# k of a pair in one load, first masks from ScalarE's queue, fewer zero products, counts behind a burst, an own h bank for the last block's odd chunks

## The chip, the cores and the metric

One core of a Trainium2 chip runs the kernel alone. Its engines are TensorE (PE: matmul, with the weight load shown as PEld), VectorE (DVE), ScalarE (ACT), GpSimd (POOL) and SyncE (SP), which here only issues DMAs. The metric is the device time of one execution in microseconds (us).

## The reference

Three stages follow each other; what is computed is this, with B, H, S, D = 4, 8, 576, 64 and 2304 tokens of 512 numbers.

```python
scores = np.matmul(q, k.transpose(0, 1, 3, 2)) / np.sqrt(D)
mask = (rel >= 0) & (rel < 128)                  # rel = query position - key position
scores = np.where(mask, scores - slope[h] * abs(rel), -1e9)
attn = softmax(scores)                           # exp of score - max, over its sum + 1e-9
x = (attn @ v), heads side by side               # [2304, 512]

h = x @ w_in                                     # [2304, 2048], w_in and w_out in double precision
g = s * np.maximum(h, 0) ** 2 + b
x = (g @ w_out).astype(np.float32)               # [2304, 512]

do = x @ w_skip > 0                              # 1360 of the 2304 rows with these inputs
e = argmax(x @ w_gate), gate = softmax(x @ w_gate)[e]      # 8 experts
out = x;  out[do] += gate * (np.maximum(x[do] @ w1[e], 0) @ w2[e])
```

With these inputs the experts 0 to 7 get 639, 194, 63, 83, 51, 20, 167 and 143 rows, which is 5, 2, 1, 1, 1, 1, 2 and 2 tiles of 128 rows.

## The kernel before, in words

**Attention** works on units: one batch, one pair of heads, and one of two halves of the queries. A unit has two or three groups (128 queries of the pair, against up to 256 keys). For a group, `qk` makes the scores of both heads (TensorE, `s_ps`), `low` adds the mask and finds the row's limit (VectorE, L179), `soft` takes exp (ScalarE, L187), sums, inverts (L189, L190) and multiplies (L196 on VectorE, L194 on ScalarE), `tr` transposes the result (TensorE, `t_ps`), `tr_ev` copies it out (ScalarE), and `pv` multiplies by v (`o_ps`). The product of `low` and `soft` is the tile `tp`, of which there are two buffers: `low` of group i+2 waits until `tr` has read group i.

The first 12 groups (phase 0) run as steps, `attn_step`, before any block of the next stage. `load_unit` issues a unit's q, k, v from SyncE's queue, the masks among the first three units, in the order of the code: for unit 0 in two pieces. k lies in memory once for each half of the partitions, so that the array holds each head's k twice in a row (`_arrays`). Ahead of the first group stand five products of zeros (`idle`), and five more follow `attn_step(2)`, each after the last score product by an issue-after mark (L703).

**The dense stage** has 6 blocks of 384 tokens, and each block 16 chunks m of 128 hidden units. `g1` makes the hidden chunk (12 products into the bank `h`, `h_ps`), ScalarE takes relu (L485), VectorE the square times s (L486), and `g1_split` splits it in a high and a low part (L495 on ScalarE, L496 on VectorE). `g2` adds the previous chunk's 9 products to the accumulators `acc0` to `acc2`. Weights come as 64-bit words and are split by `w_split` on VectorE (L412, L414, L416, L77) and ScalarE (L419): seven pieces during the attention steps 6 to 12, the rest within block 0. Attention of the later phases is woven into the blocks 0 to 4 by `events`: a `burst` (scores of two groups, `pv2` of the two before) and then a `turn` for each group (transpose and copy), at places that are fractions of the block's chunks.

**Routing** of block j-1 (`logits`, `route`) runs in block j. `route` stops half way at a `yield`: the counting products (`p_ps`, two small matmuls in the bank `at`, the same bank as `t_ps`) come later, in block j+1 behind `g1` of chunk 1. VectorE reads `p_ps` at L619 and L621.

**The experts** follow in `moe2`: expert weights stream through buffers (`ring`, `more`), are split by ScalarE (L681) and VectorE (L77), and each expert runs either `single` (one tile) or `pair` (two tiles), chosen by a branch on its count. `x_t` transposes gathered rows into the bank `p_x` (L835). `FURTHER` says how many copies of the two-more-tiles body stand in the code behind a branch that is taken only when an expert has more tiles than its first pair.

The order on an engine is set by a list scheduler, in part from its own time estimates; a chain of issue-after marks (`mm`, `order`) fixes most of TensorE's order from block 0 on, and `moe2` is scheduled by hand from `wide(0)` on. Of the change, these lines of before are touched:

```python
for c0, c1 in ((0, 128), (128, 384)) if u == 0 else ((0, 384),):   # unit 0 in two pieces
...
for _ in range(5):                                                  # zero products behind step 2
...
ts = [at + n_seg / n * f for f in ((0.55, 1) if j else (0.65, 0.85))]
...
i = g1_part(m, (3,) if j == 0 and m < 2 else range(4))              # bank "h" always
...
if counting and m == 1:
    next(counting, None)
...
x_t(rows1[0], 1)                                                    # into p_x
```

Of the kernel before, what the change touches and what calls it, by code (L numbers as in the profile page):

```python
# [17 lines left out]
B, H, S, D = 4, 8, 576, 64  # L18
# [4 lines left out]
NB = NT // TB  # L23
# [6 lines left out]
UB = 3  # L30
CONV = (6, 7, 8, 9, 10, 11, 12)
LAST = NE - 1
FURTHER = (2, 0, 0, 1, 0, 0, 0, 0)

# [6 lines left out]
def body(tc, q_in, k_in, vl, wm, we, wg, wgt, s_in, b_in, mask_in, cst_in, rout_in, ids_in, out):  # L43
    nc = tc.nc
# [11 lines left out]
    cst = main.tile([128, 4, 128], F32, name="cst")  # L56
# [27 lines left out]
    NQ, K0, NK = (384, 192), (0, 256), (384, 320)  # L84
    units, groups, ends = [], [], []
# [17 lines left out]
    def load_unit(u):  # L103
        if u >= len(units):
            return
        b, pair, half = units[u]
        q = A.tile([128, NQ[half]], F32, name="q", tag="q", bufs=UB)
        k = A.tile([128, NK[half]], F32, name="k", tag="k", bufs=UB)
        vt = A.tile([128, 2, 3, D], F32, name="vt", tag="vt", bufs=UB)

        for c0, c1 in ((0, 128), (128, 384)) if u == 0 else ((0, 384),):
            cq, ck = slice(c0, min(c1, NQ[half])), slice(c0, min(c1, NK[half]))
            nc.sync.dma_start(out=q[:, cq], in_=q_in[b, pair, :, half * 384 + cq.start:half * 384 + cq.stop])
            for i in range(2):
                rows = slice(64 * i, 64 * i + 64)
                uload[u] = nc.sync.dma_start(
                    out=k[rows, ck], in_=k_in[b, 2 * pair + i, rows, half * 384 + ck.start:half * 384 + ck.stop])
            if u < 3 and c0 == 0:
                hs = slice(2 * u, 2 * u + 2 if u < 2 else H)
                nc.sync.dma_start(out=masks[:, hs], in_=mask_in[hs].rearrange("h p n -> p h n"))  # L120
        us[u] = q, k, vt
        if u == 0:
            nc.sync.dma_start(out=cst[:, 0], in_=cst_in[:, 0])

        late.append(lambda: nc.sync.dma_start(
            out=vt, in_=vl[b, 2 * pair:2 * pair + 2, :, half * 3:half * 3 + 3].rearrange("h p t d -> p h t d")))
        while late and u:
            late.pop(0)()
# [216 lines left out]
    def events(j, n_seg):  # L345

        first, last = (ends[j] // 2, ends[UNTIL[j]] // 2)
        n, ev, wait = last - first, [], 0
        if j == 0:
            wait = 2  # L350
            n_seg -= wait
            ev.append((wait, turn, groups[2 * first - 1]))
        for i in range(n):
            d, at = first + i, 1 + wait + i * n_seg / n
            ev.append((at, burst, d))
            gs = groups[2 * d:2 * d + 2]
            ts = [at + n_seg / n * f for f in ((0.55, 1) if j else (0.65, 0.85))]
            if ceil(ts[0]) == ceil(ts[1]):
                ev.append((ts[1], turn2, gs))
            else:  # L360
                ev += [(t, turn, g) for t, g in zip(ts, gs)]
        return sorted(ev, key=lambda e: e[0])
# [116 lines left out]
        return i  # L479

    def g1(j, m):
        i = g1_part(m, (3,) if j == 0 and m < 2 else range(4))
        hp = hs[m]
        r = M.tile([128, TB], F32, name="r", tag="r", bufs=1)
        nc.scalar.activation(out=r, in_=hp, func=ACTF.Relu)  # L485
        nc.vector.scalar_tensor_tensor(out=r, in0=r, scalar=sb[:, 0:1], in1=r, op0=ALU.mult, op1=ALU.mult)  # L486
        gt[j, m] = r
        return i
# [209 lines left out]
    for i in range(ends[0]):  # L698
        attn_step(i)
        if i == 2:  # L700
            for _ in range(5):
                with tc.issue_after(pe['q'].ins):
                    pe['q'] = nc.tensor.matmul(idle[:, 0:128], lhsT=zero, rhs=zero, start=True, stop=True)  # L703
        if i == 8:
            nc.sync.dma_start(out=cst[:, 1:], in_=cst_in[:, 1:])
            nc.sync.dma_start(out=sb[:, 0:1], in_=s_in.unsqueeze(0).to_broadcast([128, 1]))
            nc.sync.dma_start(out=sb[:, 1:2], in_=b_in.unsqueeze(0).to_broadcast([128, 1]))
            nc.sync.dma_start(out=rc, in_=rout_in)
            nc.sync.dma_start(out=ids, in_=ids_in)
            nc.sync.dma_start(out=wg_sb, in_=wg)  # L710
        w_fetch()
        while w_at[1] < len(CONV) and CONV[w_at[1]] <= i:
            w_step()
# [6 lines left out]
    nc.gpsimd.memset(fill[:, 1::2], 0)  # L720
    nc.sync.dma_start(out=lst.rearrange("(p n) c -> p (n c)", p=128), in_=fill)

    counting = None
    for j in range(NB):
        if j:
            split_x(j)
        if j == NB - 1:
            ast.close()
            R = mk("moe2", ast, side="right", reuse_waits="tile")
            ws.free.extend(R.tile([128, 1024], F32, name=f"ring{i}") for i in range(RING))  # L730
            pump()
            later = moe2(tc, locals_ns(locals())).send
        todo = events(j, 2 * NM - 2) if j < UNTIL[j] else []

        def attn_until(k):
            while todo and todo[0][0] <= k:
                _, f, what = todo.pop(0)
                f(what)

        for m in range(NM):  # L740
            if j == 0:
                w_need(m)
                if m == 0:

                    g1_part(0, range(3))
                    with tc.issue_after(pe['o'].ins):
                        i = g1_part(1, range(3), "acc0")
                    order[0] = i.ins
            i = g1(j, m)
            if counting and m == 1:  # L750
                next(counting, None)
                counting = None
            attn_until(2 * m + 1)
            done = g1_split(j, m)
            if j == 0:
                w_step()
            if m:

                if j == NB - 1 and m == NM - 1:
                    g2(j, m - 2, (1, 2))  # L760
                g2(j, m - 1, (0,) if j == NB - 1 and m == NM - 2 else (0, 1, 2))
            elif j:
                g2(j - 1, NM - 1)
                evac(j - 1)
            attn_until(2 * m + 2)
            if j == 0:
                w_step()
            if j and m >= 1:
                n = 2 if j < NB - 1 else 3

                with tc.issue_after(done.ins):
                    for i in range(min(9 * TPB, n * m - n), min(9 * TPB, n * m)):
                        logits(j - 1, i)
                if m == (NM - 1 if j < NB - 1 else 10):
                    counting = route(j - 1)
                    next(counting, None)
            if j == NB - 1 and m in (10, 15):
                later(None)
            if j == NB - 1:
                split()  # L780
# [28 lines left out]
def moe2(tc, L):  # L809
# [147 lines left out]
    def pair(e, rows0, rows1, k):  # L957

        left = rest(e if e == 0 else e - 1)
        own = [p for p in NEED[e] if p[0] == e] if e else []  # L960
        x_t(rows1[0], 1)
        conv(own, 2)
        second(e - (e > 0))
        fin(1, *left)
# [188 lines left out]
```

## Time and profile before

| | |
|---|---|
| median of 3 runs | 742.35 us (739.86 to 742.79) |
| profiled execution | 742.56 us; its span 740.8 us, so 1.76 us lie around the span |
| TensorE busy | 718.6 us, 97% of the span |
| VectorE busy | 522.1 us, 70% |
| ScalarE busy | 373.9 us, 50% |
| GpSimd busy | 62.7 us, 8% |
| DMA | 96.42 MB, mean 130 GB/s |

The stages in time: attention steps from 0 to about 44 us, block 0 to about 135 us, blocks 1 to 5 to about 544 us, experts to about 730 us, and then the end of the program. An engine's busy time is the time covered by its instructions; matmul ends are modelled, so what tells most of TensorE are the gaps between its instructions, and by how much a product starts later than the one before it lets it.

### The profile page before, as it was taken

How to read it: one execution, taken by the hardware profiler on the slowest of the kernel's cores; microseconds unless marked ns; L12 is line 12 of the kernel's file. 1: busy time of each engine (PE TensorE's matmuls, PEld its weight loads, DVE VectorE, ACT ScalarE, POOL GpSimd, SP SyncE). 2: the span in 40 equal slices, each digit the busy share in tenths (PEclk: the TensorE clock that was granted, in tenths of full speed). 3: DMA queues.
4: the chain of work that ended last, by engine and by line, in shares of the span. 5: the costliest groups of instructions: out<-in, count | busy, mean ns of one | idle time of the engine just before them, and what ended most of it. 6: DMA issues, size and time to landing. Idle time of an engine off the chain costs nothing. (4 is left out here: it accounts for less than half of the span.)

```text
span 740.8 us, 13066 instructions
## 1 busy us (share of the span) xinstructions
PE 718.6 (97%) x4552; PEld 616.5 (83%) x4552; DVE 522.1 (70%) x1544; ACT 373.9 (50%) x889; POOL 62.7 (8%) x67
## 2 busy tenths in 40 slices
PE   8789999999999999999999999999999999999995
PEld 6468888888888888788888888898888889887994
DVE  4999999667777676777777665699744253999341
ACT  5776777544554444555555332454442133888230
POOL 0000000000001000000000100010105301322011
PEclk9789999999999999999999999999999999999998
DMA  7897342522314121432223111456463532999000
GB/s 194 263 345 228 128 119 54 155 65 84 94 56 131 54 68 54 132 93 70 70 80 111 30 43 31 158 170 170 127 201 81 214 114 70 344 367 386 13 22 17
DMA packets 51360, 96.42 MB, mean 130 GB/s; under 512 B 8938, under 2 KB 26858, under 8 KB 51264
## 3 DMA queue, kind: packets, MB, share of 16 engines
q1 hardware_dynamic: 46192, 86.35, 36.8%
q0 software_dynamic: 3296, 5.60, 2.4%
q10 hardware_dynamic: 1776, 3.28, 1.2%
q8 instruction: 50, 0.82, 0.5%
q14 instruction: 46, 0.38, 0.2%
HBM read 84.89 MB, written 13.65 MB: 133 GB/s over the span
## 5 line engine op out<-in xcount | busy, mean ns | idle before, releaser
L145 PE MATMUL h_ps<-xh,wh 128*128 128x384 f32 x378 | 130.9, 346 | 0.7 <-ACT r L485 0.7
L145 PE MATMUL h_ps<-xl,wh 128*128 128x384 f32 x378 | 127.5, 337 | 0.1
L145 PE MATMUL h_ps<-xh,wl 128*128 128x384 f32 x378 | 127.3, 337 | 0.0
L485 ACT ACTIVATE r<-h_ps 128x384 f32<-128x384 f32 x96 | 47.0, 490 | 134.6 <-PE h_ps L145 113.1
L486 DVE SCALAR_TENSOR_TENSOR r<-r,sb 128x384 f32<-128x384 f32 x96 | 59.1, 616 | 59.1 <-ACT r L485 58.6
L547 DVE CUSTOM_DVE_ANT_0 junk<-x,hp 128x512 bf16<-128x512 f32 x135 | 92.8, 687 | 1.6
L145 PE MATMUL acc<-wh,gh 128*128 128x512 f32 x288 | 87.0, 410 | 0.0
L187 ACT ACTIVATE tp<-tp,stat 128x256 f32<-128x256 f32 (+2 forms) x160 | 74.7, 469 | 19.8 <-DVE stat L179 19.7
L145 PE MATMUL acc<-wh,gl 128*128 128x512 f32 x288 | 83.0, 396 | 0.0
L145 PE MATMUL acc<-wl,gh 128*128 128x512 f32 x288 | 82.5, 394 | 0.0
L495 ACT ACTIVATE gh<-r,sb 128x384 fp32r<-128x384 f32 x96 | 59.2, 616 | 41.5 <-DVE r L486 40.9
L496 DVE SCALAR_TENSOR_TENSOR gl<-r,sb,gh 128x384 fp32r<-128x384 f32 x96 | 59.0, 615 | 28.2 <-ACT gh L495 28.0
L145 PEld LDWEIGHTS h_ps<-xh,wh 128*128 128x128 f32 x378 | 71.0, 188 | 6.8 <-issue 2.7
L145 PEld LDWEIGHTS h_ps<-xl,wh 128*128 128x128 f32 x378 | 71.1, 188 | 3.1 <-DVE xl L77 0.4
L145 PEld LDWEIGHTS h_ps<-xh,wl 128*128 128x128 f32 x378 | 70.9, 188 | 0.0
L145 PEld LDWEIGHTS acc<-wh,gl 128*128 128x128 f32 x288 | 54.0, 189 | 13.6 <-DVE gl L496 0.9
L145 PEld LDWEIGHTS acc<-wl,gh 128*128 128x128 f32 x288 | 54.1, 188 | 12.6
L655 POOL DMA_INDIRECT lst<-pay,di x18 | 18.5, 1028 | 489.9 <-DVE di L652 486.0
L179 DVE CUSTOM_DVE_ANT_0 tp<-s_ps,masks 128x256 f32<-128x256 f32 (+2 forms) x160 | 52.6, 377 | 9.6 <-PE s_ps L143 4.1
L145 PEld LDWEIGHTS acc<-wh,gh 128*128 128x128 f32 x288 | 50.3, 190 | 7.8 <-issue 2.9
L870 PE MATMUL p_o<-wh,hth 128*128 128x512 f32 x120 | 48.6, 405 | 0.3 <-ACT hth L886 0.2
L870 PE MATMUL p_o<-wl,hth 128*128 128x512 f32 x120 | 47.4, 395 | 0.0
(170 smaller groups left out, 1256.0 us busy)
## 6 DMA issues: line engine op xcount, KB each, us to landing
w_words<-wm SPq DMA_DIRECT2D x30, 512.0 KB, 6.3
more<-we SPq DMA_DIRECT2D x30, 512.0 KB, 6.6
ring<-we SPq DMA_DIRECT2D x28, 512.0 KB, 4.5
hp<-wgt SPq DMA_DIRECT2D x45, 256.0 KB, 3.3
vt<-vl SPq DMA_DIRECT2D x32, 192.0 KB, 3.0
x2d<-x SPq DMA_DIRECT2D x17, 256.0 KB, 2.9
out<-x SPq DMA_DIRECT2D x17, 256.0 KB, 2.8
more<-we ACTq DMA_DIRECT2D x6, 512.0 KB, 6.1
```

What stands on the lines that cost most here:

```text
L145: i = f(*args, **kw)
L179: anchor['v'] = nc.vector.tensor_tensor_reduce(out=t[0:nr, i, c0:c0 + n], in0=ps[i][0:nr, c0:c0 + n], in1=masks[0:nr, 2 * units[u][1] + i, ...
L187: anchor['s'] = nc.scalar.activation(out=t[0:nr, i, c0:c0 + n], in_=t[0:nr, i, c0:c0 + n], func=ACTF.Exp, scale=-1.0, bias=st[0:nr, 0, i:i ...
L485: nc.scalar.activation(out=r, in_=hp, func=ACTF.Relu)
L486: nc.vector.scalar_tensor_tensor(out=r, in0=r, scalar=sb[:, 0:1], in1=r, op0=ALU.mult, op1=ALU.mult)
L495: nc.scalar.activation(out=gh, in_=r, func=ACTF.Identity, bias=sb[:, 1:2])
L496: i = nc.vector.scalar_tensor_tensor(out=gl, in0=r, scalar=sb[:, 1:2], in1=gh.bitcast(F32), op0=ALU.add, op1=ALU.subtract)
L547: nc.vector.tensor_tensor_reduce(out=junk, in0=x2t[j, t], in1=w, scale=1.0, scalar=0.0, op0=ALU.mult, op1=ALU.add, accum_out=lgs[j][:, t, ...
L655: i = nc.gpsimd.indirect_dma_start(out=lst, out_offset=bass.IndirectOffsetOnAxis(ap=di[:, t:t + 1], axis=0), in_=pay[:, t, :], in_offset=N ...
L870: last = nc.tensor.matmul(p_o[s], lhsT=h[:, c, s * 128:s * 128 + 128], rhs=w[p, 4 + c // 2][:, o:o + 512], start=cs[0] == 0 and n == 0, st ...
```

## The change

- **k of a pair in one load, no split of unit 0.** A unit's q is one DMA, and its k one DMA of 128 partitions: the rows of the second copy of the pair's first head and the first copy of its second head follow each other in memory.
- **First masks from ScalarE's queue.** The masks of the pairs 0 and 1 and the identity (`cst`) are issued by ScalarE instead of SyncE; the masks of the other pairs stay with SyncE.
- **Fewer zero products**: three in place of five behind `attn_step(2)`.
- **Counts behind a burst.** The counting products of a block's routing are made behind the first burst of the block two later (past event time 2), and at chunk 1 only where no event is left (block 5).
- **Last burst**: the turns of the very last burst stand at 0.65 and 0.85 of its share instead of 0.55 and 1.
- **Own h bank**: in block 5 the odd chunks' `h_ps` is in the bank `as0`.
- **x_t of a pair's second tile** goes into `p_h[1]` instead of `p_x`.
- **FURTHER** holds three copies for expert 0 (two before), one for expert 2 (none) and none for expert 3 (one).

```diff
-FURTHER = (2, 0, 0, 1, 0, 0, 0, 0)
+FURTHER = (3, 0, 1, 0, 0, 0, 0, 0)
...
-        for c0, c1 in ((0, 128), (128, 384)) if u == 0 else ((0, 384),):
-            cq, ck = slice(c0, min(c1, NQ[half])), slice(c0, min(c1, NK[half]))
-            nc.sync.dma_start(out=q[:, cq], in_=q_in[b, pair, :, half * 384 + cq.start:half * 384 + cq.stop])
-            for i in range(2):
-                rows = slice(64 * i, 64 * i + 64)
-                uload[u] = nc.sync.dma_start(
-                    out=k[rows, ck], in_=k_in[b, 2 * pair + i, rows, half * 384 + ck.start:half * 384 + ck.stop])
-            if u < 3 and c0 == 0:
-                hs = slice(2 * u, 2 * u + 2 if u < 2 else H)
-                nc.sync.dma_start(out=masks[:, hs], in_=mask_in[hs].rearrange("h p n -> p h n"))
+        nc.sync.dma_start(out=q, in_=q_in[b, pair, :, half * 384:half * 384 + NQ[half]])
+        uload[u] = nc.sync.dma_start(out=k, in_=k_in[b].rearrange("h p n -> (h p) n")[
+            256 * pair + 64:256 * pair + 192, half * 384:half * 384 + NK[half]])
+
+        if u < 3:
+            hs = slice(2 * u, 2 * u + 2 if u < 2 else H)
+            (nc.scalar if u < 2 else nc.sync).dma_start(out=masks[:, hs], in_=mask_in[hs].rearrange("h p n -> p h n"))
+        if u == 0:
+            nc.scalar.dma_start(out=cst[:, 0], in_=cst_in[:, 0])
         us[u] = q, k, vt
-        if u == 0:
-            nc.sync.dma_start(out=cst[:, 0], in_=cst_in[:, 0])
...
-            ts = [at + n_seg / n * f for f in ((0.55, 1) if j else (0.65, 0.85))]
+            ts = [at + n_seg / n * f for f in ((0.55, 1) if j and 2 * d + 2 < len(groups) else (0.65, 0.85))]
...
-        i = g1_part(m, (3,) if j == 0 and m < 2 else range(4))
+
+        i = g1_part(m, (3,) if j == 0 and m < 2 else range(4), "as0" if j == NB - 1 and m % 2 else "h")
...
-            for _ in range(5):
+            for _ in range(3):
...
+        def count(now):
+            if counting and now:
+                next(counting.pop(), None)
+
         def attn_until(k):
             while todo and todo[0][0] <= k:
                 _, f, what = todo.pop(0)
                 f(what)
+                if f is burst:
+                    count(k > 2)
...
-            if counting and m == 1:
-                next(counting, None)
-                counting = None
+
+            count(m == 1 and not todo)
...
-                    counting = route(j - 1)
-                    next(counting, None)
+                    counting.append(route(j - 1))
+                    next(counting[0], None)
...
-        x_t(rows1[0], 1)
+        x_t(rows1[0], 1, p_h[1])
```

What the scheduler makes of it is seen in the order of the built programs. First place: SyncE's queue from the program's start, before (q, k, `vt` are a unit's inputs, `cst` the identity, `w_words` the dense stage's weights).

```order
L113 DMA q<-q_in 128x128
L116 DMA k<-k_in 64x128 x2
L120 DMA masks<-mask 128x2x256
L113 DMA q<-q_in 128x256
L116 DMA k<-k_in 64x256 x2
L123 DMA cst<-cst 128x128
L113 DMA q<-q_in 128x384
L116 DMA k<-k_in 64x384 x2
L120 DMA masks<-mask 128x2x256
L125 DMA vt<-vl 128x2x192 x2
```

The same queue in the changed program:

```order
L111 DMA q<-q_in 128x384
L112 DMA k<-k_in 128x384
L111 DMA q<-q_in 128x384
L112 DMA k<-k_in 128x384
L121 DMA vt<-vl 128x2x192 x2
```

Twelve issues ahead of the first `vt` have become four; the first two masks and `cst` now stand first on ScalarE's queue, ahead of its table load.

TensorE at the same place, before (`idle` are the zero products):

```order
L143 MATMUL idle<-pt 128x128 x5
L143 MATMUL s_ps<-k,q 128x128 x2
L143 MATMUL s_ps<-k,q 128x256 x4
L703 MATMUL idle<-pt 128x128 x5
L143 MATMUL t_ps<-cst,tp 128x128 x2
L143 MATMUL s_ps<-k,q 128x128 x2
L143 MATMUL t_ps<-cst,tp 128x128 x4
```

and in the changed program:

```order
L139 MATMUL idle<-pt 128x128 x5
L139 MATMUL s_ps<-k,q 128x128 x2
L139 MATMUL s_ps<-k,q 128x256 x4
L700 MATMUL idle<-pt 128x128 x3
L139 MATMUL s_ps<-k,q 128x128
L139 MATMUL t_ps<-cst,tp 128x128
L139 MATMUL s_ps<-k,q 128x128
L139 MATMUL t_ps<-cst,tp 128x128 x5
```

Two zero products are gone, and the scores of group 3 stand between the transposes of group 0's two heads.

Second place: VectorE at the start of block 0, before (`wl`, `hp`, `w_words`: weight pieces; `r`, `gl`: the hidden chunk; the `tp` of 128x256 is the last step's group).

```order
L77 TENSOR_TENSOR wl_510<-hp,wh_509 128x512
L412 TENSOR_SCALAR hp<-w_words 128x512
L190 RECIPROCAL stat<-stat 128x2
L486 SCALAR_TENSOR_TENSOR r<-r,sb 128x384
L414 SCALAR_TENSOR_TENSOR hp<-w_words,hp 128x512
L196 TENSOR_SCALAR tp<-tp,stat 128x256
L416 SCALAR_TENSOR_TENSOR hp<-w_words,hp 128x512
L496 SCALAR_TENSOR_TENSOR gl<-r,sb,gh 128x384
```

and in the changed program:

```order
L186 RECIPROCAL stat<-stat 128x2
L77 TENSOR_TENSOR wl_499<-hp,wh_498 128x512
L408 TENSOR_SCALAR hp<-w_words 128x512
L192 TENSOR_SCALAR tp<-tp,stat 128x256
L483 SCALAR_TENSOR_TENSOR r<-r,sb 128x384
L410 SCALAR_TENSOR_TENSOR hp<-w_words,hp 128x512
L412 SCALAR_TENSOR_TENSOR hp<-w_words,hp 128x512
L493 SCALAR_TENSOR_TENSOR gl<-r,sb,gh 128x384
```

The product that finishes `tp` has moved ahead of `r` and of one weight instruction. Behind `gl`, the r of chunk 1 (two rows later before) now stands behind the four L175 of the first burst and part of a weight piece.

Third place: TensorE in block 3, behind `g1` of chunk 1, before:

```order
L145 MATMUL p_ps<-oh,cst 128x24 x2
L145 MATMUL t_ps<-cst,tp 128x128 x4
L145 MATMUL acc<-wh_289,gh 128x512 x3
L145 MATMUL acc<-wl_290,gh 128x512 x3
L145 MATMUL acc<-wh_289,gl 128x512 x3
```

and in the changed program:

```order
L141 MATMUL t_ps<-cst,tp 128x128 x4
L141 MATMUL acc<-wh_280,gh 128x512 x3
L141 MATMUL acc<-wl_281,gh 128x512 x3
L141 MATMUL acc<-wh_280,gl 128x512 x3
L141 MATMUL t_ps<-cst,tp 128x64
L141 MATMUL t_ps<-cst,tp 64x64
L141 MATMUL t_ps<-cst,tp 128x64
L141 MATMUL t_ps<-cst,tp 64x64
L141 MATMUL s_ps<-k,q 64x192 x6
L141 MATMUL o_ps<-pt,vt 64x64 x4
L141 MATMUL o_ps<-pt,vt 64x128 x4
L141 MATMUL p_ps<-oh,cst 128x24 x2
```

The counting products no longer stand directly ahead of a transpose; they follow the next burst, and 12 products of the next hidden chunk come behind them.

## Rows read from the trace of the kernel before

**Rows 1.** The page, first part: busy time, share, instructions.

```profile
PE 718.6 (97%) x4552; PEld 616.5 (83%) x4552; DVE 522.1 (70%) x1544; ACT 373.9 (50%) x889; POOL 62.7 (8%) x67
```

**Rows 2.** Windows: length, engines' busy time (instructions), granted clock, DMA share, GB/s.

```profile
0.00:18.00 18.00, 15.00 (x84) 11.71 (x84) 7.97 (x41) 10.08 (x31) 0.97 (x8) 1.00 0.71 190
...
24.00:26.00 2.00, 0.41 (x2) 0.20 (x2) 2.00 (x6) 1.90 (x5) 0.00 (x0) 1.00 1.05 327
...
28.00:40.00 12.00, 10.98 (x47) 7.57 (x48) 11.59 (x40) 8.97 (x26) 0.00 (x0) 0.50 0.70 192
...
52.00:54.00 2.00, 2.00 (x12) 1.43 (x9) 1.87 (x9) 1.85 (x8) 0.00 (x0) 0.56 1.05 402
...
90.00:130.00 40.00, 40.00 (x267) 34.45 (x260) 39.22 (x108) 30.24 (x81) 0.00 (x0) 1.00 0.34 96
130.00:230.00 100.00, 100.00 (x712) 86.44 (x711) 71.18 (x271) 50.79 (x150) 0.24 (x1) 1.00 0.35 101
```

**Rows 3.** Timeline of the first steps: start, length, engine, line, idle before.

```profile
2.42 0.59 SPq L120 DMA_DIRECT2D masks<-mask  x1
...
3.54 1.27 PE L143 MATMUL s_ps<-k,q 64*128 64x128 f32 x4
...
4.95 0.29 DVE L179 CUSTOM_DVE_ANT_0 tp<-s_ps,masks 128x128 f32<-128x128 f32 x1 [2.94 <-PE s_ps L143]
...
6.36 2.31 PE L143 MATMUL s_ps<-k,q 64*128 64x256 f32 x8 [1.55 <-DMA k<-k_in]
...
8.60 2.50 PE L703 MATMUL idle<-pt 128*128 128x128 f32 x10
...
10.89 0.64 PE L143 MATMUL t_ps<-cst,tp 128*128 128x128 f32 x2
...
11.57 0.42 DVE L179 CUSTOM_DVE_ANT_0 tp<-s_ps,masks 128x256 f32<-128x256 f32 x1 [1.22 <-PE t_ps L143]
...
13.13 2.05 SPq L402 DMA_DIRECT2D w_words<-wm  x4
```

**Rows 4.** DMA issues from 0 to 20 us: count, KB each, median us to landing.

```profile
q<-q_in SPq DMA_DIRECT2D x4, 192.0 KB, 4.5
...
masks<-mask SPq DMA_DIRECT2D x2, 128.0 KB, 2.5
...
k<-k_in SPq DMA_DIRECT2D x2, 32.0 KB, 2.2
```

**Rows 5.** Timeline at the start of block 0.

```profile
47.38 0.59 DVE L486 SCALAR_TENSOR_TENSOR r<-r,sb 128x384 f32<-128x384 f32 x1
...
48.49 0.34 DVE L196 TENSOR_SCALAR tp<-tp,stat 128x256 f32<-128x256 f32 x1
...
48.98 0.63 PE L145 MATMUL t_ps<-cst,tp 128*128 128x128 f32 x4 [2.05 <-DVE tp L196]
```

**Rows 6.** Timeline of the counts in block 3.

```profile
308.59 0.52 PE L145 MATMUL p_ps<-oh,cst 128*128 128x24 f32 x4
...
310.44 0.63 PE L145 MATMUL t_ps<-cst,tp 128*128 128x128 f32 x4 [1.33 <-DVE cnt L620]
```

**Rows 7.** Timeline of the last burst's turn, in block 4.

```profile
453.85 0.45 PE L145 MATMUL t_ps<-cst,tp 64*128 64x64 f32 x4
...
454.80 1.04 PE L145 MATMUL o_ps<-pt,vt 64*64 64x64 f32 x16 [0.51 <-ACT pt L227]
```

**Rows 8.** Timeline of block 5, chunk 15.

```profile
534.41 0.86 PE L145 MATMUL acc<-wh,gh 128*128 128x512 f32 x3
...
535.46 0.49 ACT L485 ACTIVATE r<-h_ps 128x384 f32<-128x384 f32 x1 [1.36 <-DVE gl L496]
...
536.00 0.44 PE L145 MATMUL h_ps<-xh,wh 128*128 128x384 f32 x1 [0.73 <-ACT r L485]
```

**Rows 9.** Timeline of the second tile's transposes, experts 1 and 6.

```profile
607.11 0.42 PEld L835 LDWEIGHTS p_x<-cst,two 128*128 128x128 f32 x4 [0.57 <-DVE wl L77]
...
681.01 0.66 PE L835 MATMUL p_x<-cst,two 128*128 128x128 f32 x4 [0.40 <-DVE wl L77]
```

More of the change, by code (lines that the diff above doesn't have):

```diff
@@ L721, in body @@
     nc.sync.dma_start(out=lst.rearrange("(p n) c -> p (n c)", p=128), in_=fill)
-    counting = None
+    counting = []
     for j in range(NB):
@@ L749, in body @@
             i = g1(j, m)
-            if counting and m == 1:
-                next(counting, None)
-                counting = None
+            count(m == 1 and not todo)
             attn_until(2 * m + 1)
```

## The prediction

> **What bounds the kernel.** I read the busy shares first: TensorE is covered for 97% of the span, VectorE for 70% [rows 1]. A covered TensorE is not yet the bound, so I went to the windows. From 130 us on TensorE has no free time while VectorE is busy for 71 of 100 us: there TensorE is the bound. In block 0 (90 to 130 us) both are full, 40.0 and 39.2 of 40 us. Before that VectorE is full and TensorE is not (24 to 26 us: 2.00 against 0.41), and before 18 us neither is: 15.0 and 8.0 of 18 us [rows 2]. So three things can be gained: an earlier start of VectorE's full stretch, TensorE's holes at the start of block 0, and single holes of TensorE in the blocks and experts. An off-TensorE saving after 130 us is worth nothing. The third view was the timeline around each hole of TensorE over 0.3 us; the change touches seven of them.
>
> Next, the first steps [rows 3]. The first masked scores (L179) run at 4.95 us, when the mask that SyncE issued at 2.42 us has come (128 KB need 2.5 us [rows 4]). Group 1's scores start only at 6.36 us, waiting for the second piece of k. Behind group 2's scores ten zero-product instructions hold TensorE from 8.60 to 10.89 us; only then come the transposes of group 0, and L179 of group 2, which needs group 0's buffer of `tp`, starts at 11.57 us as soon as they end. From there each pair of steps depends on the one before by those two buffers, so what L179 of group 2 gains is kept until VectorE is full, and then shifts its whole queue.
>
> **The start.** SyncE's queue holds four issues ahead of the first v where twelve stood, and ScalarE has three new ones ahead of its table load. Three issues at 0.59 us (the mask's row) are 1.8 us of ScalarE, which has nothing to do before L179 at 4.95 but its table load: nothing, as long as that load takes under 2.5 us. The first q and k are now 192 KB each. For k's landing the rows give 2.2 us (32 KB, quiet) and 4.5 us (192 KB, in heavy traffic); I take 2.8 us, close to the 2.5 us of the 128 KB mask issued at the same time. With k issued at about 1.2 us, group 0's scores start at 4.0 us, half a us later than 3.54. But group 1 needs no further load. Eight score instructions took 2.24 us (6.36 to 8.60), four half as wide at most 1.1; so group 0 ends at 5.0, group 2 at 7.2 us. Ten zero instructions took 2.29 us, six take 1.4: 8.6 us. One head's scores of group 3 stand between the two transposes now, some 0.4 us beside their 0.64: group 0 is read at 9.6 us, and L179 of group 2 starts then in place of 11.57: **2.0 us**. Of these, 0.9 come from the two zero products, the rest from loads. Bounds: with k landing after 4.5 us group 1 starts no sooner than before and only the zero products count (0.8 us); with 2.2 us it is 2.6, and 3.0 if the four narrow score instructions cost half of what I gave. The weights, first issued at 13.13 us, move up in SyncE's queue by more than this, so the first split finds them.
>
> A rule of the Trainium skill bears on the masks. The rows show SyncE issuing one DMA per 0.4 to 0.6 us, and a DMA share of 0.71 over the first 18 us [rows 2, 3]. The page "DMA: Bandwidth & Descriptors" (section "Issuing engines are not separate DMA queues") says that DMAs started by different engines run on the same 16 DMA engines, so a second queue saves issue time alone. By that rule the masks on ScalarE's queue share bandwidth with k, and 2.8 us is fair; were the queue a road of its own, the start would be at the 2.6 us end.
>
> **Start of block 0.** TensorE waits 2.05 us for L196, which stands behind r and L414 [rows 5]. It moves ahead of both: 48.49 less 47.38 is 1.1 us. The hole shrinks by 1.1 us, if TensorE then finds work; VectorE is full there and its total work is unchanged, so part returns as a later wait. I take half, **0.6 us**, bounds 0 and 1.1. The r of chunk 1, now behind four L179 and a weight piece, is the likely place of return (a rival, below).
>
> **Counts.** The four counting products of block 3 end at 309.12 us, and the transposes behind them need the same bank, which VectorE has read only at 310.4: 1.33 us of idle TensorE [rows 6]. In the new order hidden-chunk products stand there, and the next transpose is half a burst away: **1.3 us**, bounds 0.9 and 1.4 (VectorE, stalled inside a burst, could hand 0.4 on). In the blocks 2, 4 and 5 accumulator products already stood behind the counts: nothing.
>
> **Last burst.** Its last transposes move ahead of nine accumulator products, so the 0.51 us in which `o_ps` waited for the copy [rows 7] lie beside those nine (three take 0.86 us at most [rows 8]): **0.5 us**. Its `tp` is a burst's work of more than half a share earlier; bounds 0 (if it is not ready) and 0.5.
>
> **h bank.** In chunk 15 of block 5 TensorE idles 0.73 us, as the only h bank is held until relu at 535.46, itself late behind VectorE [rows 8]. Chunk 15 is odd: it gets `as0`, whose last reader was chunk 13's relu. **0.7 us**; bounds 0.2 (if the gathered rows for the transposes six us later then end last) and 0.9. Other odd chunks of block 5 show no hole.
>
> **x_t.** The second tile's transposes wait for VectorE to read the same bank: 0.40 us at expert 6, and at expert 1 up to the 0.57 us that the weight load idles, which runs ahead of its product [rows 9]. `p_h[1]` was read long before. 0.35 and 0.3: **0.65 us**, bounds 0.3 and 0.97. For the experts 0 and 7 no hole was seen.
>
> **FURTHER.** No expert has more than 5 (expert 0) or 2 tiles, so these bodies are jumped over before and now: the branch target lies farther for the experts 0 and 2 and nearer for 3. Nothing, bounds -0.3 and 0.3.
>
> **The sum.** 2.0 + 0.6 + 1.3 + 0.5 + 0.7 + 0.65 = 5.8 us off the profiled execution's 742.56 us (span 740.8 and 1.76 around it): **736.7 us**. The median shown is 0.2 lower than that execution; I leave that inside the range. What is late next: TensorE itself, everywhere from 56 us on.
>
> **Rivals.** A, *the clock stays up in block 0*: at 52 to 54 us TensorE is covered but at a granted clock of 0.56 [rows 2], after the idle stretch that shrinks. If it stays at 2.4 GHz, some 4 us at half speed cost 1.7 us less: 735.0 us. For it: the hole before gets 1.1 us smaller. Against: half of that hole stays.
>
> B, *block 0 takes the start back*: both engines are full at 90 to 130 us, and r of chunk 1 comes later by four L179 (0.42 and 0.29 us for the two widths [rows 3], 1.4 us) and by weight instructions of the length of r and L196, 0.3 to 0.6 us each, two or three of them: 2.4 to 3 us. If TensorE has to wait for that chunk's g, the 2.6 us of the start are gone: 742.56 - 3.2 = 739.4 us. For it: VectorE has no slack. Against: the products of chunk 0's g and of the next hidden chunk stand ahead of it on TensorE.
>
> C, *the clock falls in the first steps* (the other side): with fewer zero products TensorE drops to 1.2 GHz at about 9 us and stays there to 18 us. By the rows it was busy 15.0 of 18 us at clock 1.00, of these 6.1 before 8.60 (scores 1.27 and 2.31, and the first five zero products like the second, 2.50 [rows 3]); the other 8.9 us double, 3.0 us of free time absorb a third, and 5.9 us are lost while the 2.0 are not gained: 742.56 - 3.8 + 5.9 = 744.7 us. It decides as soon as more than 5.8 us are added. For it: at 24 to 26 us TensorE was busy for 0.41 us, and the clock stood at 0.50 from 28 to 40 us [rows 2]. Against: the gaps of the first 18 us get shorter by more than the zero products shrink. The Trainium skill says the same of the clock in "TensorE: Matmul & The Clock Gate" (section "HAM oscillation — how this bites in real kernels"): gaps of an idle TensorE bring its clock down to half. The trace agrees for the gap at 24 us; by that rule taking out zero products is a risk, and it is case C alone.
>
> **Numbers.** Under 0.5% (3.7 us, so 738.6 us is the edge) a measurement of this kernel can't tell a difference. The sum as forecast (736.7, itself 735.5 to 738.4): 0.50. A (735.0): 0.20. B (739.4): 0.20. C (744.7): 0.07. Elsewhere, on either side of the old time: 0.03. Faster: 0.48 of the first, all of A, a fifth of B, 0.72 together. Same: the rest of these, 0.19. Slower: C and a part of the last, 0.09. Range: from 733.6 (A, with the start and block 0 at their upper ends: 1.5 us more) to 740.7 (B, with the later terms near their lower ends: 1.3 us less).
>
> **What would show it.** Right: L179 of group 2 near 9.6 us; first weight issue before 11 us; no idle TensorE behind the counts of block 3, ahead of chunk 15, ahead of the last `o_ps` and ahead of the second tiles of experts 1 and 6; at any later place the same work about 2.6 us earlier in block 1 and 5.8 us earlier at the end. Wrong: group 0's scores after 5 us; granted clock below 1.00 before 18 us; block 1 starting less than 1 us earlier although the steps end 2 us earlier; or the holes closed in blocks and experts with the same idle time at the next product.

## The result, and the profile after

The changed kernel takes 736.27 us (median of 6 runs, 735.23 to 737.19); the kernel before, run beside it, 742.53 us. The ratio is 0.992, with a 95% interval of 0.9904 to 0.9937. The profiled execution took 737.19 us, 5.4 us less than the one of before (its span 735.3, 5.5 us less). The sum of the prediction, 5.8 us, came out, but not by its terms alone: in this pair of profiles the start and block 0 gave 1.7 us less than forecast, and a change of the clock that was no term gave 1.5 us.

The first part of the page, to set beside [rows 1]; TensorE's busy time fell by 2.7 us only, so the other half of the 5.5 is idle time that went.

```profile
PE 715.9 (97%) x4548; PEld 614.6 (84%) x4548; DVE 521.3 (71%) x1544; ACT 373.7 (51%) x889; POOL 62.7 (9%) x67
```

Windows of the changed kernel, columns as in [rows 2]. The DMA share of the first 18 us rose from 0.71 to 0.90; the half-speed stretch of block 0's start (0.56 at 52 to 54 us before) lies at 48 to 50 us now; and from 90 to 130 us TensorE has free time that it had not.

```profile
0.00:18.00 18.00, 15.53 (x82) 11.34 (x84) 8.16 (x42) 10.16 (x33) 0.97 (x8) 1.00 0.90 273
28.00:40.00 12.00, 10.38 (x46) 7.58 (x46) 11.56 (x40) 8.59 (x24) 0.00 (x0) 0.50 1.04 380
48.00:50.00 2.00, 2.00 (x11) 1.56 (x15) 1.97 (x4) 1.59 (x3) 0.00 (x0) 0.50 0.33 131
52.00:54.00 2.00, 2.00 (x11) 1.65 (x10) 2.00 (x8) 1.90 (x10) 0.00 (x0) 1.00 0.84 280
90.00:130.00 40.00, 39.26 (x241) 33.29 (x240) 39.70 (x104) 29.57 (x78) 0.00 (x0) 1.00 0.30 92
```

The timeline of its first steps, against [rows 3]:

```profile
4.56 2.58 PE L139 MATMUL s_ps<-k,q 64*128 64x128 f32 x12 [1.06 <-DMA k<-k_in]
...
7.07 1.65 PE L700 MATMUL idle<-pt 128*128 128x128 f32 x6
...
8.65 0.79 PE L139 MATMUL s_ps<-k,q 64*128 64x128 f32 x2
...
9.54 2.25 SPq L398 DMA_DIRECT2D w_words<-wm  x4
...
10.50 1.33 PE L139 MATMUL t_ps<-cst,tp 128*128 128x128 f32 x5
...
11.01 0.42 DVE L175 CUSTOM_DVE_ANT_0 tp<-s_ps,masks 128x256 f32<-128x256 f32 x1 [1.70 <-PE t_ps L139]
...
11.76 0.70 PE L261 MATMUL o_ps<-pt,vt 128*64 128x128 f32 x4
```

All scores of the groups 0 to 2 run without a break, and the weights are issued 3.6 us earlier. But L175 of group 2 starts at 11.01 us, not at 9.6. Between 8.65 and 11.0 us stand one head's scores, one transpose, the other head's scores, and the other transposes; and they are slow: two score rows take 0.79 us, where two of the same kind take 0.48 from 16 us on, and four `o_ps` take 0.70 against 0.44 later. That is TensorE at its lower level, 1.2 GHz, though the granted clock in the windows reads 1.00: two such score rows take the same 0.79 us at 33.45 us, where the column reads 0.50. In the first 20 us the column does not show the lower level, the products' own lengths do.

Three places of the chain after it, against [rows 5] to [rows 8]: the transposes at the start of block 0, those of block 3 that stood behind the counts, and chunk 15 of block 5.

```profile
47.87 1.09 PE L141 MATMUL t_ps<-cst,tp 128*128 128x128 f32 x4 [0.85 <-DVE tp L192]
...
307.70 0.60 PE L141 MATMUL t_ps<-cst,tp 128*128 128x128 f32 x4
...
452.10 1.04 PE L141 MATMUL o_ps<-pt,vt 64*64 64x64 f32 x16
...
532.41 0.34 PE L141 MATMUL h_ps<-xh,wh 128*128 128x384 f32 x1
```

The wait of 2.05 us is 0.85 us; the other three rows have no wait any more. How much earlier the same TensorE work stands, place by place (times of the kernel before), tells what each was worth in this pair of executions:

| up to | earlier by, us | gained there |
|---|---|---|
| L175 of group 2 (VectorE) | 0.56 | |
| last steps (33 us) | 0.40 | |
| 46.5 us, ahead of block 0's first transposes | -0.08 | |
| 54 us, behind them | 1.17 | |
| 74 us | 2.27 | |
| 92 us | 2.36 | |
| block 1 (r at 131.20, before 132.07) | 0.87 | start and block 0: 0.87 |
| block 3, behind the counts (340 us) | 2.33 | counts: 1.46 |
| block 4, behind the last burst | 2.70 | last burst: 0.37 |
| block 5, chunk 15 | 3.66 | h bank: 0.96 |
| 565 us, behind the routing of the last block | 5.15 | unforeseen: 1.49 |
| 625 us, behind expert 1 | 5.48 | x_t, expert 1: 0.33 |
| end | 5.45 | x_t, expert 6: 0 |

Most of the gain at 74 us is a wait of 0.66 us for `tp` at 73.34 us that is gone. Of the 2.4 us at 92 us, 1.5 are lost again at three products that take `wl`, at 107.2, 112.6 and 119.3 us of the changed kernel (0.80, 0.24 and 0.48 us):

```profile
107.22 0.45 PE L141 MATMUL h_ps<-xh,wl 128*128 128x384 f32 x1 [0.53 <-DVE wl L77]
...
119.25 0.44 PE L141 MATMUL h_ps<-xh,wl 128*128 128x384 f32 x1 [0.20 <-DVE wl L77]
```

The unforeseen 1.49 us is the clock. Windows of the kernel before and then of the changed one, at the same work, behind the `l_ps` products of the last routing:

```profile
552.00:554.00 2.00, 2.00 (x6) 1.56 (x5) 1.60 (x15) 0.06 (x1) 0.00 (x0) 0.53 0.70 274
```

```profile
548.00:550.00 2.00, 2.00 (x11) 1.59 (x10) 1.90 (x17) 0.22 (x1) 0.00 (x0) 1.00 0.57 220
```

TensorE is covered in both, but six products fit where eleven do now: before, it went to 1.2 GHz at 552 us for some 3 us, with the same products at the same distances ahead of it.

At expert 6 the bank `p_h[1]` lets the transposes start at once, and the next product waits instead:

```profile
675.00 0.60 PE L837 MATMUL p_h<-cst,two 128*128 128x128 f32 x4
675.42 0.74 DVE L877 SCALAR_TENSOR_TENSOR og<-p_o,la,one 128x512 f32<-128x512 f32 x1
...
676.32 0.47 PE L872 MATMUL p_o<-wh,hth 128*128 128x512 f32 x1 [0.72 <-DVE og L877]
```

It writes the bank that `og` is being read from. The 0.40 us of [rows 9] have moved one product on.

### The profile page after: what moved, and what is told of

The parts are those of the page before. It is cut to its first block, busy times and chain, and to the rows that moved or that the text cites. A ratio compares the mean times of both kernels' runs of the same rounds, so it can differ in the third digit from the quotient of the medians.

```text
span 735.3 us, 13013 instructions
## 1 busy us (share of the span) xinstructions
PE 715.9 (97%) x4548; PEld 614.6 (84%) x4548; DVE 521.3 (71%) x1544; ACT 373.7 (51%) x889; POOL 62.7 (9%) x67
## 5 line engine op out<-in xcount | busy, mean ns | idle before, releaser
L175 DVE CUSTOM_DVE_ANT_0 tp<-s_ps,masks 128x256 f32<-128x256 f32 (+2 forms) x160 | 52.6, 378 | 8.9 <-PE t_ps L139 3.8
```

The costliest lines, as they stand in the source:

```text
L175: anchor['v'] = nc.vector.tensor_tensor_reduce(out=t[0:nr, i, c0:c0 + n], in0=ps[i][0:nr, c0:c0 + n], in1=masks[0:nr, 2 * units[u][1] + i, ...
```

## The experiments

Two things were open: why the lead of 2.4 us in block 0 became 0.87, and whether the h bank has to do with the clock at 552 us. "V" is the theory that VectorE, not TensorE, sets the time up to about 125 us.

**order3.** The scores of group 3 behind both transposes of group 0 (an issue-after mark):

```diff
-                pe['q'] = mm(nc.tensor.matmul, ps[i][...
+                with tc.issue_after(pe['t'].ins) if gi == 3 else ExitStack():
+                    pe['q'] = mm(nc.tensor.matmul, ps[i][...
```

> The changed kernel, in which the scores of group 3 stand behind both transposes of group 0 instead of between them; the three zero products stay. Both theories: the transposes start at 8.65 us, when the zero products end, and L175 of group 2 at 9.4 to 9.7 us (11.01 in the changed kernel). Theory V (VectorE is what bounds the time from 18 to about 125 us, so that all that reaches its queue early is kept): r at the start of block 1 (131.20) 1.0 to 1.6 us earlier, profiled time 735.6 to 736.2. Theory T (TensorE's half-speed stretch in the steps sets the pace, and block 0 takes the start back): r at the start of block 1 within 0.3 us of 131.20, profiled time 736.9 to 737.5.

Median 732.98 us (732.63 to 735.42), ratio to the kernel before 0.9881 [0.9866, 0.9897]: 3.3 us less than the changed kernel, more than V asked. The timeline:

```profile
8.59 0.64 PE L139 MATMUL t_ps<-cst,tp 128*128 128x128 f32 x2
9.15 0.80 PE L139 MATMUL s_ps<-k,q 64*128 64x128 f32 x4
9.30 0.42 DVE L176 CUSTOM_DVE_ANT_0 tp<-s_ps,masks 128x256 f32<-128x256 f32 x1
```

L176 of group 2 starts as soon as VectorE is free, 1.7 us earlier than in the changed kernel. Some 0.8 us of that are the order: vector_more, below, has the changed kernel's order at full speed, and L175 there at 10.07 us. The rest is the half speed of the changed kernel's profile, which did not come here. Block 1 begins at 127.35 us, 3.85 earlier, and all of it is kept to the end.

**order0.** As order3, and `range(3)` of the zero products is `range(0)`.

> As the run before it, and without the three zero products behind step 2. The transposes of group 0 wait for its product on ScalarE (8.04) instead of for zero products, L175 of group 2 starts at 9.3 us behind L192 of group 1. Theory V: 0.1 to 0.4 us less than the run before it, granted clock 1.00 up to 18 us. Theory C (the zero products hold the clock up): granted clock at 0.5 somewhere between 7 and 18 us, and 3 us more than the run before it.

Median 738.66 us (0.9953 [0.994, 0.9966]), 5.7 us over order3. Theory C is right in what it does, though not by the clock column, which reads 1.00 up to 30 us. Rows of eight `o_ps`, first at half speed, then at full speed:

```profile
17.75 1.12 PE L264 MATMUL o_ps<-pt,vt 128*64 128x128 f32 x8
...
24.84 0.66 PE L264 MATMUL o_ps<-pt,vt 128*64 128x128 f32 x8
```

The products are at half speed from 7.7 us, behind a gap of 0.42 us, to 23 us. VectorE then waits 3.04 us at 13.5 and 1.69 at 20.8 us for scores, and block 1 begins at 133.18.

**vector_more.** `lower(wl...)` twice for the weight pieces 20, 22, 24 and 26.

> The changed kernel, in which four weight pieces of block 0 (those of the chunks 10 to 13) have their low part made twice by VectorE: four instructions of 0.65 us, 2.6 us more of VectorE's work and none of TensorE's. Theory V: TensorE waits longer for wl from 100 to 125 us, r at the start of block 1 1.3 to 2.6 us later, profiled time 738.5 to 739.8. Theory T, and the prediction's own claim that from 56 us on TensorE is what is late: under 0.5 us later.

Median 740.76 us (0.9964 [0.9949, 0.998]): 4.5 us more for 2.6 us of VectorE's work, beyond what V asked. The timeline shows the first new wait, and the windows what follows it:

```profile
107.32 0.62 PE L141 MATMUL h_ps<-xh,wl 128*128 128x384 f32 x1 [1.32 <-DVE wl L77]
```

```profile
106.00:108.00 2.00, 0.68 (x3) 0.68 (x3) 1.97 (x4) 1.97 (x5) 0.00 (x0) 0.86 0.00 0
108.00:110.00 2.00, 2.00 (x8) 2.00 (x8) 2.00 (x5) 0.00 (x0) 0.00 (x0) 0.50 0.00 0
```

VectorE stays full, TensorE waits for `wl`, and after the wait runs at half speed. Block 1 begins 3.5 us later. TensorE stood 1.7 us ahead of the changed kernel's profile at 100 us and stands 2.9 us behind it from 130 us on: 4.6 us lost in that stretch. The twelve executions spread from 736.1 to 741.77 us, and two of them lie inside the changed kernel's range, so the added work does not cost every execution the same. Still, nothing of it was absorbed here: the prediction's claim that TensorE is what is late from 56 us on is wrong for the changed kernel, and V holds there, up to the last wait for `wl` (119 us in the changed kernel). One program can also differ: this one is the changed kernel's up to 60 us, and its first products ran at full speed (two score rows in 0.48 us), L175 of group 2 at 10.07.

**load_only.** The kernel before with the new `load_unit`, five zero products.

> The kernel before with the new loads alone: a unit's k in one DMA, the first masks and the identity from ScalarE's queue, five zero products as before; L196 of the last step stays behind r at the start of block 0. Theory V (up to about 125 us VectorE's work and idle time set the time): L175 of group 2 at 10.4 to 11.0 us in place of 11.57, block 1 (r at 132.07) earlier by as much as VectorE has idled less, 0.2 to 1.2 us, the start of block 0 notwithstanding. Rival P (the place of L196 is what the changed kernel gained before block 1): r at the start of block 1 within 0.2 us of 132.07.

L175 of group 2 at 11.25 us (expected 10.4 to 11.0), block 1 at 130.60, 1.47 us earlier; VectorE had idled 1.09 us less. L175 shows nothing: counts_only and bank_only, below, have the old start and L179 of group 2 at 11.18 and 11.45 us. Block 1 begins 0.85 us ahead of the earliest of the three profiles with the old start (131.45), with L196 in its old place; that speaks against P, and V asked for no more than 1.2. One profile does not show that the loads alone bring something. In time it is unclear: median 741.39 us, ratio 1.0 [0.9978, 1.0022], with two of eleven executions at 747.52 and 747.74 us.

**xt_old.** `x_t(rows1[0], 1)` in the changed kernel.

> The changed kernel with x_t of the second tile in p_x again. Theory H (what p_h gives at expert 6 is taken back by the next product, which waits for og to be read from the one bank p_o): 0.2 to 0.4 us lost at expert 1 and 0.1 us or less at expert 6. Rival, the prediction's: 0.3 and 0.35, together 0.65 us. Up to 560 us it is the same program as the changed kernel, and so shows what differs between two executions of it: products at half speed in the first steps or none, L175 of group 2 between 10.0 and 11.1 us.

Median 737.33 us (0.9936 [0.9923, 0.9948]). Against the changed kernel 0.34 us are lost at expert 1 and nothing at expert 6, as theory H has it; another 0.45 us go at the first product of the next expert, whose weight load waits 0.71 us for nothing that the profile shows. bank_not15, below, has that wait too (0.67 us) with the new bank of x_t, so it is not x_t's. Up to 560 us the program is the changed kernel's, yet block 1 begins at 129.10, 2.1 us earlier: products were at half speed at 9 to 14 us as there, but the stretch of 27 to 41 us ended at 32, and the one at 48 us did not come.

**order5.** As order3, with five zero products.

> The run order3 with five zero products behind step 2 in place of three. L175 of group 2 at 9.7 to 9.9 us (9.30 there), products at full speed from 9 to 20 us. Theory V: block 1 begins 0.3 to 0.7 us later than in order3 (127.35), profiled time 733.6 to 734.0. Rival (three zero products hold the clock only sometimes, five always): the executions spread less than in order3 (732.6 to 735.4), and their median is no higher than 733.0.

L176 of group 2 at 9.24 us, block 1 at 128.78, 1.4 later than in order3, with half speed up to 39 us and again at 46. The median, 738.49 us, fits neither theory: 3.6 us are lost at 663 us, at the first product of expert 5, and another 1.4 at half speed behind it. The timeline there, weight load and product:

```profile
663.62 0.29 PEld L850 LDWEIGHTS p_h<-wh,xth 128*128 128x128 f32 x1 [3.61 <-issue]
...
663.65 0.76 PE L850 MATMUL p_h<-wh,xth 128*128 128x512 f32 x1 [3.40 <-DVE wl L77]
```

The `wl` named had ended at 660.6 us, and for its weight load TensorE waited for nothing that the profile shows.

**order5_again and order3_again**, the same two kernels once more.

> The kernel of the run order5 once more. In its profile TensorE waited 3.40 us for its first p_h product at 660 us, which no other profile shows. If that wait belongs to the program (its instructions lie elsewhere in memory), it shows again at the same product and the median is 737.5 to 739 us. If it was one execution's, the median is 734 to 736 us and the profile shows no wait over 1 us behind 560 us.

Median 739.06 us; the wait is back at the same product, and the products behind it are at half speed:

```profile
661.38 0.29 PEld L850 LDWEIGHTS p_h<-wh,xth 128*128 128x128 f32 x1 [3.22 <-issue]
661.41 0.77 PE L850 MATMUL p_h<-wh,xth 128*128 128x512 f32 x1 [3.01 <-ACT wh L681]
661.98 0.63 PE L850 MATMUL p_h<-wl,xth 128*128 128x512 f32 x1
```

It belongs to the program. Block 1 began at 126.49, the earliest of all (128.78 in order5), so no harm of five zero products to the start is seen; the wait takes back more than they could bring.

> The kernel of the run order3 once more, since executions of one program begin block 1 up to 3.8 us apart (the changed kernel's program at 131.20, 130.64, 129.10 and 127.38 us). Theory V (the order is worth it in every execution, as the transposes need no luck with the clock): L175 of group 2 at 9.3 to 9.4 us again, block 1 from 127.0 to 129.0 us, median 732.5 to 734.0 us. Rival L (order3 was lucky executions): median 735.5 to 736.5 us, as the changed kernel, 736.27.

Median 733.24 us (732.62 to 733.37), ratio 0.988 [0.9866, 0.9895], L176 of group 2 at 9.35, block 1 at 127.53. Theory L is out: this version beats both kernels.

**counts_only.** The kernel before with the new `count` and its three calls.

> The kernel before with the counts behind a burst alone. Theory H (the idle time behind the counts is the whole of it): TensorE does not wait behind the counts of block 3 (1.33 us before), the work from 312 us on is 1.2 to 1.5 us earlier than in the kernel before, offsets of the first 130 us aside. Rival: VectorE, stalled inside the burst by the two reads of the counts, hands it on: under 0.6 us. Apart from both, the half-speed stretch at 552 to 555 us of the kernel before may or may not show.

Median 740.55 us (0.9972 [0.9962, 0.9982]). The work of block 3 moves from 0.24 us later to 1.21 earlier, 1.45 us; theory H.

**bank_only.** The kernel before with `"as0" if j == NB - 1 and m % 2 else "h"`.

> The kernel before with the own h bank for the odd chunks of block 5 alone. Theory H (the bank is worth its hole, and the rest of what block 5's end gained is the clock, which has nothing to do with the bank): the 0.73 us ahead of chunk 15 go, the work from 541 to 550 us is 0.7 to 1.0 us earlier, and the half-speed stretch at 552 to 555 us either stays (profiled time 741.6 to 741.9) or falls elsewhere by chance. Theory K (the idle 0.73 us of chunk 15 are what lets the clock fall 16 us later): granted clock 1.00 from 545 to 560 us and 2.2 to 2.5 us less, 740.1 to 740.4.

Median 740.63 us (0.9986 [0.9975, 0.9996]). At chunk 15 the lead over the kernel before grows from 0.55 to 1.54 us; 0.67 of these 0.99 us are given back six us later:

```profile
540.82 0.63 PE L835 MATMUL p_x<-cst,two 128*128 128x128 f32 x4 [0.47 <-DMA two<-x2d,la]
```

That is the case of the prediction's lower bound, rows that end last. The half-speed stretch at 552 us did not come, worth another 1.5 us; two more runs were to tell whether the bank did that.

**bank_not15 and bank_15.** The changed kernel with `m % 2 and m < 15`, and with `m == 15`.

> The changed kernel with the own h bank for the odd chunks 1 to 13 of block 5, but not for chunk 15. So far all three profiles without the own bank (the kernel before, counts_only, load_only) show TensorE at half speed at 550 to 555 us, and one of seven with it (vector_more). Theory K (the idle time ahead of chunk 15 goes with the half-speed stretch 16 us later): an idle 0.7 us ahead of chunk 15, half speed for about 3 us behind the l_ps products, and 2 us more than in the run bank_15, of which 0.7 to 0.9 by 541 us and 1.2 to 1.5 at the stretch. Theory H (the stretch is chance, and has nothing to do with the bank): the idle 0.7 us, and the stretch as likely here as in bank_15.

> The changed kernel with the own h bank for chunk 15 alone. Both theories: no idle time ahead of chunk 15, block 5 as long as in the changed kernel within 0.1 us, so that the other seven odd chunks gain nothing. Theory K: no half-speed stretch at 545 to 555 us. Theory H: as likely as in bank_not15. It is the changed kernel's program up to block 5, and shows once more whether products run at half speed between 8 and 14 us: if so, L175 of group 2 at 11.0 to 11.2 us, if not at 10.0 to 10.2.

Medians 737.64 us (0.9941 [0.9923, 0.9959]) and 735.35 us (0.9915 [0.9903, 0.9928]). Without the bank for chunk 15 the idle time is back, and there is no half speed behind it:

```profile
532.62 0.44 PE L141 MATMUL h_ps<-xh,wh 128*128 128x384 f32 x1 [0.73 <-ACT r L482]
```

```profile
550.00:552.00 2.00, 2.00 (x15) 1.55 (x13) 1.13 (x9) 1.06 (x2) 0.00 (x0) 1.00 0.22 85
```

Against the changed kernel 0.96 us are lost at chunk 15. vector_more is the reverse, the bank and no idle time, but half speed:

```profile
552.00:554.00 2.00, 2.00 (x6) 1.52 (x5) 0.93 (x9) 0.00 (x0) 0.00 (x0) 0.50 0.15 53
```

So theory K is out as it stands: neither needs the other. 4 of the 14 profiles have the stretch: before, counts_only and load_only, which lack the bank, and vector_more, which has it. That is 3 of 4 with the idle time ahead of chunk 15 and 1 of 10 without; whether the bank makes the stretch rarer, and what lets it come, stays open. bank_15 is as fast in block 5 as the changed kernel: chunk 15 is the bank's whole worth. The 2.3 us between the two medians are more than chunk 15; in the profiles block 1 began at 130.64 and at 127.38 us.

## Why the prediction was right, and where it was not

**V in numbers.** VectorE's idle time from the start to the first r of block 1 (the sum of the gaps between its instructions, semaphore waits counted as gaps), and when that r starts:

| kernel | idle, us | r of block 1 at | difference |
|---|---|---|---|
| before | 15.00 | 132.07 | 117.07 |
| after | 14.54 | 131.20 | 116.66 |
| load_only | 13.91 | 130.60 | 116.69 |
| xt_old | 12.70 | 129.10 | 116.40 |
| bank_15 | 11.12 | 127.38 | 116.26 |
| order3 | 11.04 | 127.35 | 116.31 |
| order5_again | 10.10 | 126.49 | 116.39 |
| order0 | 16.72 | 133.18 | 116.46 |

The idle time differs by 6.6 us and the work by 0.8. That alone does not say which engine sets the time: what an engine has idled and what it has worked add up to the place it has reached, for every engine. It says that these starts of block 1 differ by VectorE's idle time, and so where to look. VectorE idles in the first 17 us, waiting for scores, and later where TensorE at half speed is late with them. In the changed kernel that is at 51.22 us:

```profile
51.22 0.43 DVE L175 CUSTOM_DVE_ANT_0 tp<-s_ps,masks 128x256 f32<-128x256 f32 x1 [1.11 <-PE s_ps L141]
```

That VectorE's work sets the time is shown for the changed kernel, by vector_more and by the waits for `wl` up to 119 us. In the kernel before it does not hold that far: TensorE has no gap over 0.15 us from 73.34 us on, and it is VectorE that waits, 2.58 us for the relu at the first r of block 1 (1.29 us in the changed kernel):

```profile
132.07 0.62 DVE L486 SCALAR_TENSOR_TENSOR r<-r,sb 128x384 f32<-128x384 f32 x1 [2.58 <-ACT r L485]
```

**The sum.** The terms add up to 736.8 us; 736.7 is a slip of 0.1. The profiled 737.19 us lie near it because two misses cancel: 1.7 us too much for the start and block 0, and 1.5 us of clock that no term had.

**The start and block 0: the step that failed.** The prediction gave 2.0 + 0.6 us; the pair of profiles shows 0.87. Its own sign of being wrong came, block 1 less than 1 us earlier. The zero products end at 8.65 us, as forecast (8.6), but by two errors that cancel. "I take 2.8 us" for k: the first k landed 3.2 us after its issue, with the first masks beside it at 3.1 (2.5 before, [rows 4]), and the first scores came at 4.56 instead of 4.0 us. The landings of the issues of the first 1.5 us:

```profile
k<-k_in SPq DMA_DIRECT2D x1, 192.0 KB, 3.2
masks<-mask ACTq DMA_DIRECT2D x1, 128.0 KB, 3.1
```

The twelve score instructions then took 2.5 us, where the prediction had 3.2. The page "DMA: Bandwidth & Descriptors" of the Trainium skill (section "Issuing engines are not separate DMA queues") has all engines' transfers interleave on the same 16 DMA engines; the slower masks fit that, but no run moves them alone.

What failed is the step behind the zero products, "some 0.4 us beside their 0.64". The other head's scores stand ahead of the first transpose too, as the order of the changed program shows, and the prediction did not count them: scores and transposes take from 8.62 to about 10.0 us at full speed (vector_more), from 8.65 to 11.0 at half speed. So L175 of group 2 came at 10.07 to 11.20 us in five profiles of this program, not at 9.6; only the order of order3 reached that. Nor is its gain kept as it is: xt_old has L175 at 11.20 and block 1 at 129.10 us, the changed kernel 11.01 and 131.20.

In block 0 the hole shrank by 1.2 us, as said, and TensorE stood 1.2 us further ahead behind it; the wait at 73 us gave 1.1 more, which no term had. What failed is "TensorE itself, everywhere from 56 us on": 1.5 us of the lead were lost again where TensorE waits for `wl`. That is rival B where it saw both engines full, though not through r of chunk 1.

Yet the term is nearer to the truth than this pair. Four profiles of this start (after, bank_not15, xt_old, bank_15) begin block 1 at 131.20, 130.64, 129.10 and 127.38 us, mean 129.6; three of the old one (before, bank_only, counts_only) at 132.07, 131.45 and 132.31, mean 131.9. That is 2.4 us, with a spread in the new start that one profile cannot tell. Which edit brought how much of it is not settled.

**Rivals A and C.** Both came in part. The half speed at 52 us did not go, it moved to 48 us, where VectorE waits for the scores; in xt_old, bank_not15 and bank_15, the same program up to there, it is gone. C's drop in the first steps came in three of the five profiles of this start (not in vector_more and bank_15), for 4 to 8 us of the 9 that it named; without zero products it lasted to 23 us. The Trainium skill says in "TensorE: Matmul & The Clock Gate" (section "HAM oscillation — how this bites in real kernels") that an idle TensorE loses its clock; order0 agrees in that the products fell to half speed when the zero products were gone, but the gap just ahead was only 0.42 us, and in the changed kernel half speed began at 8.65 us with no gap over 0.15 us since 4.56. The same page (section "Seeing it yourself") calls the recorded events of the clock unreliable; the windows that read 1.00 beside products of 0.70 in place of 0.44 us agree with that too. The condition of C, "granted clock below 1.00 before 18 us", was therefore one that could not have shown it.

**Counts.** Right: 1.3 predicted, 1.46 and 1.45 measured. **Last burst**: 0.5 predicted, 0.37. **h bank**: right in mechanism; 0.7 predicted, 0.96 here and by bank_not15, 0.32 left of 0.99 in bank_only, where the gathered rows end last. **x_t**: expert 1 right (0.3 predicted, 0.33); expert 6 failed (0.35 predicted, nothing): the same idle time at the next product, the sign that the prediction had named, since that product needs a bank that VectorE is reading at that moment; the prediction asked who reads the transposes' bank, not who reads the next product's. **The clock at 552 us** was no term; it made up for the start. **FURTHER**: no run tells.

## What to carry to other kernels

Where two engines are both full, add a little work to one of them before calling the other the bound. Summing one engine's idle time up to a place tells where two variants differ, not which engine sets the pace. Look at what stands between a freed wait and the instruction that is to gain by it: the score products around two transposes held L175 back by 0.8 us at full speed and by more at half speed, and with them moved behind the median fell by 3 us. And where the clock falls differently from one execution to the next, compare several executions place by place before a term of 1 us is called right or wrong.

## What was not expected of the hardware

Programs that are the same up to block 5 begin block 1 up to 3.8 us apart, by where TensorE falls to half speed and for how long; order5's program, run twice, 2.3 us apart, order3's 0.2. Two more zero products at the program's start (order5 against order3) cost 3.0 and 3.4 us of waiting at the first product of expert 5, and half speed after it; smaller waits of the kind (0.30 us in xt_old) stand at the first product of another expert. In the code these products are the first of an expert, behind the branch on its count. The Trainium skill has, in "Runtime: NRT & Kernel Launch" (section "🔬 Instruction fetch mechanics"), that a taken branch whose target is not loaded waits for the code to be fetched; the trace fits, as the wait has no other releaser and the two instructions move the code behind them, but no run here separates it from anything else.
